# Float32 P·V for two tiles in place of four and a half, in whole 128-row pieces, with exponentials of four tiles kept in PSUM

## The chip, the cores and the metric

One core of a Trainium2 chip. The metric is the device time of one execution in microseconds (us), the median over several runs. Engines are named as in the profile: PE is TensorE, PEld its weight load, DVE is VectorE, ACT is ScalarE, POOL is GpSimd, SP is SyncE, which issues every DMA here.

## What is computed

Attention with rotary positions over 4 batches, 8 heads, 576 rows and 64 columns a head, then a two-layer network with a parametric ReLU on all 2304 rows. All inputs and outputs are float32 (the weights come to the chip as 64-bit words and are converted there).

```python
scores = matmul(rot(q), rot(k).T) / sqrt(64)
attn = exp(scores - max(scores))
attn = attn / (sum(attn) + 1e-09)
x = matmul(attn, v)                       # to [2304, 512]
h = x @ w_in                              # 512 -> 2048
g = maximum(h, 0) + alpha * minimum(h, 0)
out = g @ w_out                           # 2048 -> 512
```

## The kernel before

**Tiles and blocks.** The 2304 rows are 18 tiles of 128 rows, two tiles to a block. A batch has 576 rows, so batch 0 is tiles 0 to 3 and the first half of tile 4 (called 4a here, its other half 4b). Attention of a tile goes by pairs of heads (`pair`): both heads' scores go into two PSUM buffers of the tag `pair` (L766), then each head goes on by itself (`head`): the row maximum on DVE (L814), the exponential with its sum on ACT (L818), and P·V. For a half tile (`half_pair`) the two heads' 64 rows stand in one buffer of 128 partitions, so the work up to P·V is done once for both.

**Two ways for P·V.** Batch 0 goes the float32 way (`head_f32`): five PE transposes write the exponentials back into the same PSUM buffer (L858), a copy on ACT or DVE brings them to SBUF (L868, L869), and five float32 matmuls with 128, 128, 128, 128 and 64 rows give P·V (L863). PE runs each float32 matmul as two instructions, so one head is 10 instructions of L863. The other batches go the split way: P is scaled and written as a float16 part (`p_hi`, L827 on ACT, L829 through the helper of L460 on DVE) and a float16 remainder (`p_lo`, L831, DVE), SP issues a DMA transpose of both (`p_turn`, L835), and 14 float16 matmuls with V's own two parts give P·V (L842). V is split once a batch: its largest value on ACT or DVE (`v_max`), a short chain for the scale (`v_bound`), the parts (`v_hi`, L554, ACT; `v_lo`, L558, DVE) and two small DMAs a pair of heads (`v_shift`). For batch 0 the scale alone is formed, before tile 4.

**The network.** Blocks 0 and 1 run it in float32 (L929 the first layer, L956 the second), with 16 steps j a block. Each j is L929, then on ACT and DVE the activation (L947, L950), then L956. From block 2 on it runs with split float16 weights and inputs (L936, L974). There is one PSUM buffer for a first-layer result, so the next j's first layer waits for L950 of this one.

**What runs beside what.** Attention of tiles 0 and 1 runs alone. Then attention of block i+1 runs beside the network of block i, on the same engines. In blocks 0 and 1 the weights are also loaded (L609), converted by three DVE operations each (L591, L596, L600), and later split into two float16 parts (L669 to L677 and L687 to L691).

**The order.** The whole program is planned ahead: `Plan.run` simulates five engines, and an engine that is free takes the ready operation with the lowest key, which is its due time plus an offset from the tables `OFF` and `PEN`. What an engine executes is fixed in that order, SP's queue included. [...]

**PSUM.** There are three buffers of the tag `pair`, one `v` and one `h`. Beside the network one `pair` buffer holds the second layer's sums and attention has the other two. In the float32 way a buffer is free after the copy of L868 or L869; in the split way after the exponential, which goes to an SBUF buffer `e` (two of them).

Of the kernel before, what the change touches and what calls it, by code (L numbers as in the profile page):

```python
# [37 lines left out]
NB, NF = 1, 2  # L38
# [5 lines left out]
    "a_bound": [34.01],  # L44
    "alpha": [-62.66],
    "beta": [139.98],
    "eps": [-27.34],
    "exp": [79.08, 81.69, -20.81, 118.21, 156.27, -106.7, 113.18, 210.0, -10.34],
    "eye": [-64.76],
    "f_copy": [-31.64, -37.36, -102.13],  # L50
    "f_pv": [4.79, -100.55, 119.9],
    "f_turn": [124.68, -7.54, 47.11],
    "gh": [-121.31, -121.31, -209.6, -195.84, -162.63, -294.46, -186.23, -108.51, 43.31],
    "gl": [-108.2, -108.2, -125.9, -107.83, -164.4, -121.69, -183.9, -105.22, -107.42],
    "k_add": [-6.37, -107.42, -77.63, -62.38],
    "k_hi": [-17.31, 206.39, 65.35, -11.75],
    "k_lo": [-8.45, 101.55, 60.72, -91.74],
    "k_load": [-121.58, -5.26, 126.18, -177.4],
    "k_mul": [60.28, 5.5, 144.31, 120.8],
# [3 lines left out]
    "norm": [-30.88, -90.24, -74.41, -41.63, -82.09, -98.15, -6.94, -46.4, 90.17],  # L63
    "p_hi": [-58.14, -58.14, -74.15, 7.2, -22.71, 28.22, -32.85, -19.97, -141.27],
    "p_lo": [0.78, 0.78, -4.23, -48.72, -107.88, 120.43, -23.33, 100.96, -22.39],
    "p_turn": [-60.56, -60.56, -9.24, -181.49, -122.05, -85.88, -83.8, 1.05, -60.99],
    "prelu": [-103.2, -47.63, -208.13, -158.48, -88.74, -22.37, 44.96, 69.39, 126.15],
    "pv": [-0.07, -0.07, -58.65, 1.14, 35.89, 11.06, -9.72, 3.01, 13.88],
    "q_add": [335.99, 222.46, 352.3, 486.65, 358.5, 547.76, 421.94, 324.24, 183.36, 360.56, 277.59, 215.55, 247.18, 276.04, 353.98, 417.31, 295.01, 298.07],
    "q_hi": [79.07, 79.07, 79.07, 79.07, 79.07, 68.02, 27.89, 98.78, 75.48, 139.53, -68.85, 122.73, 33.74, 111.04, 86.24, 188.84, 327.3, 98.3],  # L70
    "q_lo": [43.6, 43.6, 43.6, 43.6, 43.6, 15.46, -1.52, -47.43, -21.1, 36.88, 86.21, -93.64, -64.6, -97.08, -232.93, -50.34, 94.96, -73.31],
    "q_load": [-36.84, -74.58, -4.21, -63.07, -133.9, -6.27, 8.43, -228.53, -218.75, -128.69, -36.92, -51.96, -68.15, -151.88, -143.73, -53.86, 29.83, 9.38],
    "q_mul": [15.75, -153.47, -6.76, 16.19, 81.64, 140.86, -12.48, 242.35, -145.86, -16.83, -95.05, -56.59, 30.24, 123.99, -64.6, 111.53, 41.76, 19.84],
    "qd_hi": [0.48, 0.48, 83.94, 76.74, 34.0, 32.87, 15.7],
    "qd_lo": [15.84, 15.84, 144.03, 14.21, 12.4, 26.43, 36.9],
    "qd_zero": [-12.23, -12.23, 17.58, 3.62, -12.96, -20.64, -130.84],
    "relu": [19.99, -79.39, -142.28, -117.18, -150.93, -198.12, -66.5, -252.61, -83.53],
    "res": [65.32, 45.86, 121.16, 21.91, 72.49, 6.0, -83.92, -21.55, 69.41],
    "scores": [-8.97, 2.78, -84.49, -37.64, -2.03, -17.61, 11.45, 33.02, -3.31],
    "store": [-82.23, -121.07, -79.43, -39.06, 109.09, 234.19, 235.51, 70.93, 189.03],  # L80
    "tab": [-148.29, -112.05],
    "v_bound": [-167.23, -131.59, -10.65, -88.48],
    "v_hi": [-18.97, -156.9, -74.24, -181.19],
    "v_lo": [-23.23, -55.85, 32.22, 25.69],
    "v_load": [-45.39, 64.43, 42.85, -44.07],
    "v_max": [125.78, 164.73, 111.8, 175.9],
# [1060 lines left out]
```

## Time and profile before

| | us |
|---|---|
| median of 3 runs | 668.09 |
| the runs | 667.92, 668.09, 672.72 |
| the profiled execution | 670.72 |
| its span, first to last instruction | 668.9 |
| PE busy / DVE / ACT / POOL | 631.4 / 486.3 / 356.7 / 235.5 |

The page gives busy time by engine, slices of the span, the chain that ended last, and the costliest groups of instructions. A PE instruction's own duration holds a pipeline tail that overlaps the next one, so the time that a PE group takes is read from its start to the start of the next group. A count is followed by the busy time and the mean of one.

### The profile page before, as it was taken

The numbers are of one execution on the slowest core, as the hardware profiler recorded it, in microseconds if no ns is written. First come the engines' busy times: TensorE is split into PE (matmuls) and PEld (weight loads), VectorE is DVE, ScalarE is ACT, GpSimd is POOL, SyncE is SP. The second block draws the span as 40 slices with busy tenths as digits, with TensorE's granted clock in tenths as the row PEclk, the third lists the DMA queues.
The fourth block names the chain that finished last, engine by engine and source line by source line (L and its number), as shares of the span: only waits on it lengthen the run. The fifth ranks groups of instructions, "written<-read, shape, count | busy, mean of one in ns | idle before, by whom it ended". The sixth has DMA issues, their size and how long they took to land.

```text
span 668.9 us, 13924 instructions
## 1 busy us (share of the span) xinstructions
PE 631.4 (94%) x5482; PEld 451.3 (67%) x5482; DVE 486.3 (73%) x779; ACT 356.7 (53%) x792; POOL 235.5 (35%) x185
## 2 busy tenths in 40 slices
PE   1799899999999999999999999999999999999997
PEld 1578677677676666677766767777667666776664
DVE  5999688524589889887978786689867757853332
ACT  2386555422497665755676555477445555633322
POOL 3767200001077853564855352138621211210000
PEclk9989999999999999999999999999999999999999
DMA  8953555001145876577978586287645828860000
GB/s 307 403 202 115 222 202 190 1 1 31 68 134 135 137 137 105 134 138 150 210 140 193 112 166 110 52 158 172 130 52 105 145 48 115 155 97 1 31 2 33
DMA packets 162130, 84.29 MB, mean 126 GB/s; under 512 B 144912, under 2 KB 148624, under 8 KB 162064
## 3 DMA queue, kind: packets, MB, share of 16 engines
q1 hardware_dynamic: 162064, 83.39, 54.1%
q8 instruction: 43, 0.70, 0.4%
q14 instruction: 23, 0.19, 0.1%
HBM read 41.56 MB, written 4.72 MB: 69 GB/s over the span
## 4 chain that ended last, share of the span: by engine, by line
PE 78%; DMA 8%; DVE 6%; ACT 4%; issue 2%; SPq 1%; DVEq 0%; ACTq 0%
PE h L936 19%; PE pair L974 18%; PE pair L766 8%; PE pair L956 8%; PE h L929 7%; PE v L863 7%; PE v L842 6%; DMA pt<-pp 6%; PE pair L858 3%; PE pair L787 2%; DMA kraw<-in_k_dram 2%; ACT e L818 1%; DVE mx L814 1%; DVE pp L831 1%; DMA out_dram<-os 1%
## 5 line engine op out<-in xcount | busy, mean ns | idle before, releaser
L936 PE MATMUL h<-xt,wi 128*128 128x256 f16 (+1 forms) x1344 | 169.5, 273 | 1.3 <-DVE r L950 1.2
L936 PEld LDWEIGHTS <-wi 128*128 128x128 f16 (+1 forms) x1344 | 127.0, 98 | 34.6 <-issue 5.3
L818 ACT ACTIVATE e<-pair,mx 128x576 f32<-128x576 f32 x144 | 105.6, 737 | 62.7 <-DVE mx L814 56.8
L974 PE MATMUL pair<-wh,gh 128*128 128x512 f16 x448 | 133.4, 379 | 0.3 <-DVE os L460 0.3
L950 DVE SCALAR_TENSOR_TENSOR r<-r,beta,h 128x256 f32<-128x256 f32 x144 | 68.5, 476 | 85.5 <-ACT r L947 84.6
L947 ACT ACTIVATE r<-h 128x256 f32<-128x256 f32 x144 | 54.7, 380 | 131.2 <-PE h L936 86.7
L967 POOL TENSOR_TENSOR gl<-r,gh 128x256 bf16<-128x256 f32 x66 | 57.6, 873 | 168.1 <-ACT gh L964 102.8
L814 DVE TENSOR_REDUCE mx<-pair 128x1 f32<-128x576 f32 x144 | 103.0, 748 | 11.5 <-PE pair L766 9.4
L831 DVE SCALAR_TENSOR_TENSOR pp<-e,pp 128x576 f16<-128x576 f32 x108 | 103.2, 962 | 8.4 <-ACT pp L827 7.7
L974 PE MATMUL pair<-wh,gl 128*128 128x512 f16 x224 | 84.9, 379 | 0.0
L842 PEld LDWEIGHTS <-pt 128*128 128x128 f16 (+1 forms) x1680 | 59.5, 101 | 18.5 <-DMA pt<-pp 8.8
L842 PE MATMUL v<-vv,pt 128*128 128x64 f16 (+1 forms) x1680 | 64.8, 194 | 6.1 <-DMA pt<-pp 4.8
L964 ACT ACTIVATE gh<-r 128x256 f16<-128x256 f32 x100 | 41.5, 415 | 46.7 <-DVE r L950 26.5
L929 PE MATMUL h<-xt,wi 128*128 128x256 f32 x256 | 64.2, 389 | 1.9 <-DVE r L950 1.2
L974 PEld LDWEIGHTS <-gh 128*128 128x128 f16 x448 | 41.2, 98 | 33.7 <-issue 2.1
L956 PE MATMUL pair<-wo,r 128*128 128x512 f32 x128 | 61.4, 602 | 0.0
L863 PEld LDWEIGHTS v<-vf,pt 128*128 128x128 f32 (+3 forms) x400 | 46.8, 179 | 15.6 <-issue 9.0
L929 PEld LDWEIGHTS h<-xt,wi 128*128 128x128 f32 x256 | 46.3, 190 | 13.8 <-issue 4.3
L863 PE MATMUL v<-vf,pt 128*128 128x64 f32 (+3 forms) x400 | 52.5, 272 | 1.2 <-ACT pt L868 1.1
L766 PE MATMUL pair<-kh,qn 64*128 64x288 f32 x576 | 51.3, 308 | 0.5 <-ACT e L818 0.5
L766 PEld LDWEIGHTS pair<-kh,qn 64*128 64x128 f32 x576 | 39.8, 184 | 15.6 <-issue 7.1
L714 POOL TENSOR_TENSOR qr<-qr,tab 128x1024 f32<-128x1024 f32 (+1 forms) x17 | 40.2, 2370 | 22.0 <-DMA qr<-in_q_dram 21.8
(121 smaller groups left out, 749.2 us busy)
## 6 DMA issues: line engine op xcount, KB each, us to landing
qr<-in_q_dram SPq DMA_DIRECT2D x17, 512.0 KB, 4.0
wraw<-in_moe_w_in_dram SPq DMA_DIRECT2D x16, 512.0 KB, 5.9
wraw<-in_moe_w_out_dram SPq DMA_DIRECT2D x16, 512.0 KB, 5.7
kraw<-in_k_dram SPq DMA_DIRECT2D x12, 576.0 KB, 4.8
out_dram<-os SPq DMA_DIRECT2D x18, 256.0 KB, 2.5
vraw<-in_v_dram SPq DMA_DIRECT2D x12, 320.0 KB, 4.3
kraw<-in_k_dram SPq DMA_DIRECT2D x8, 288.0 KB, 4.4
pt<-pp SPq DMA_TRANSPOSE x108, 3.4
```

What stands on the lines that cost most here:

```text
L766: nc.tensor.matmul(out=ps[h]()[:, x, :HS], lhsT=qn()[r, p] if b == 0 else qn()[r, i, p], rhs=kt()[r, c] if b == 0 else kt()[r, j, c], star ...
L814: lambda e: nc.vector.tensor_reduce(out=mx()[a:z], in_=ps()[a:z, :, :HS], axis=AX.XY, op=ALU.max, negate=True),
L818: lambda e: nc.scalar.activation(out=ex()[a:z].rearrange("p (x c) -> p x c", x=2), in_=ps()[a:z, :, :HS], func=ACTF.Exp, bias=mx()[a:z], a ...
L831: lambda e: nc.vector.scalar_tensor_tensor(out=pp()[a:z, 1], in0=ex()[a:z], scalar=E_SC, in1=pp()[a:z, 0], op0=ALU.mult, op1=ALU.subtract),
L842: nc.tensor.matmul(out=v_b()[c:d, 2 * p + g], lhsT=pt()[:, s, o:o + d - c], rhs=vt()[:, g, w], start=(n == 0), stop=(n == len(order) - 1))
L863: nc.tensor.matmul(out=v_b()[c:d, 2 * p + g], lhsT=pt()[:w, s, o:o + d - c], rhs=raw()[:w, g, s], start=(s == 0), stop=(s == NH - 1))
L929: nc.tensor.matmul(out=ps(), lhsT=w32(kk, j // FG)[:, f], rhs=x()[:, kk], start=(kk == 0), stop=(kk == KC - 1))
L936: nc.tensor.matmul(out=ps(), lhsT=wt.bitcast(BF16) if w else wt, rhs=xs.bitcast(BF16) if y else xs, start=(kk == 0 and n == 0), stop=(kk = ...
L950: lambda e: nc.vector.scalar_tensor_tensor(out=g(), in0=g(), scalar=beta_b()[:, j:j + 1], in1=ps(), op0=ALU.mult, op1=ALU.add),
L956: nc.tensor.matmul(out=po()[:, x], lhsT=g()[:, x * 128:(x + 1) * 128], rhs=wf[j // 2]()[:, j % 2], start=(j == 0), stop=(j == KF - 1))
L967: lambda e: ENG[e].tensor_tensor(out=gl(), in0=g(), in1=gh(), op=ALU.subtract),
L974: nc.tensor.matmul(out=po()[:, x], lhsT=s()[:, ts], rhs=w, start=(j == 0 and c == 0), stop=(j == KF - 1 and c == 2))
```

## The change

- `WHOLE = (0, 1)`: only tiles 0 and 1 go the float32 way. Tiles 2, 3 and 4a take the split way for P·V. Their scores stay in float32, and blocks 0 and 1 keep the float32 network, so y of tiles 2 and 3 is transposed by PE as before and their output gets V's scale at the end.
- V of batch 0 is therefore split too (`split_values`), at tile 2; it is loaded into the `vraw` buffers and no longer into `vv` slots.
- The float32 way has five pieces of 128 rows: the last covers the last 128 rows, of which the host lays out a sixth piece of V whose upper half is zero. So its load grows from five pieces to six.
- `IN_PLACE = (2, 3, 4, 5)`: in these tiles the exponential writes back into its PSUM buffer, and `p_hi` and `p_lo` read it there. The buffer is free after `p_lo`. [...]
- The tables `OFF`, `PEN` and the three constants behind them are new, so the order of all operations is another one.
- The case `NB`, which was 1, is taken out; it changes no order by itself.

```diff
-NB, NF = 1, 2
+NF = 2
+WHOLE = (0, 1)
+IN_PLACE = (2, 3, 4, 5)
...
-PW, LW, BACKLOG = 205.88, 49.53, 2091.5
+PW, LW, BACKLOG = 209.82, 40.46, 4570.2
...
-    rv_T = tag("vraw", NP, [128, 2, NH, D], F32)
+    rv_T = tag("vraw", NP, [128, 2, NH + 1, D], F32)
...
-            raw = vraw[b, p] = made(vv_T.new(), vv_T, [128, 2, NH, D], F32, "vf") if b == 0 else rv_T.new()
-            load("v_load", b, at, raw, 128 * 2 * NH * D * 4, raw, v[b, p])
+            n = NH + 1 if b == 0 else NH
+            raw = vraw[b, p] = rv_T.new()
+            load("v_load", b, at, raw, 128 * 2 * n * D * 4, lambda raw=raw, n=n: raw()[:, :, :n], v[b, p][:, :, :n])
...
-        mx, ex, pt = mx_T.new(), e_T.new(), pt_T.new()
+        mx, pt = mx_T.new(), pt_T.new()
+        if t in IN_PLACE:
+            ex, e_y, e_z = ps, lambda: ps()[a:z, :, :HS], lambda y: y.rearrange("p (x c) -> p x c", x=2)
+        else:
+            ex = e_T.new()
+            e_y, e_z = lambda: ex()[a:z], lambda y: y
...
-        if b == 0:
+        if t in WHOLE:
             return head_f32(i, at, t, p, sides, c, d, ex, ps, pt)
...
-        op("p_hi", i, at + 0.2, {ACT: act(S), DVE: dve(S, fast=True)},
+        op("p_hi", i, at + 0.2, {ACT: act(S, t in IN_PLACE), DVE: dve(S, fast=t not in IN_PLACE)},
...
-           reads=[ex, (pp, 0)], writes=[(pp, 1)])
+           reads=[ex, (pp, 0)], writes=[(pp, 1)], port=t not in IN_PLACE)
...
             for s in range(NH):
-                w = min(128, S - 128 * s)
-                nc.tensor.transpose(flat()[:w, 128 * s:128 * s + 128], ex()[:, 128 * s:128 * s + w], eye_b())
+                o = min(128 * s, S - 128)
+                nc.tensor.transpose(flat()[:, 128 * s:128 * s + 128], ex()[:, o:o + 128], eye_b())
...
-                w = min(128, S - 128 * s)
-                nc.tensor.matmul(out=v_b()[c:d, 2 * p + g], lhsT=pt()[:w, s, o:o + d - c], rhs=raw()[:w, g, s],
+                nc.tensor.matmul(out=v_b()[c:d, 2 * p + g], lhsT=pt()[:, s, o:o + d - c], rhs=raw()[:, g, s if s < NH - 1 else NH],
...
-            if t == 2 * NF and a == 0 and p == 0:
+            if t == WHOLE[-1] + 1 and p == 0:
                 bound_values(at, 0, bank().new())
+                split_values(at, 0)
...
+    vt = np.concatenate([vt, np.zeros_like(vt[:, :, :, :, :1])], axis=4)
+    vt[:, :, 64:, :, -1] = vt[:, :, :64, :, -2]
```

## Rows read from the trace of the kernel before

**Rows 1.** The page's first part: busy time, share of the span, instructions.
```profile
span 668.9 us, 13924 instructions
PE 631.4 (94%) x5482; PEld 451.3 (67%) x5482; DVE 486.3 (73%) x779; ACT 356.7 (53%) x792; POOL 235.5 (35%) x185
```

**Rows 2.** By stretch: us; busy PE, PEld, DVE, ACT, POOL; PEclk; DMA share; GB/s.
```profile
17.00:72.00 55.00, 48.57 (x312) 38.46 (x312) 49.98 (x46) 33.04 (x67) 36.51 (x18) 0.97 0.60 232
72.00:178.00 106.00, 104.44 (x540) 75.62 (x541) 63.78 (x94) 44.00 (x92) 5.12 (x9) 1.00 0.29 106
178.00:264.00 86.00, 83.05 (x632) 57.74 (x631) 76.24 (x130) 61.95 (x125) 53.63 (x31) 1.00 0.59 121
264.00:600.00 336.00, 328.68 (x3562) 235.69 (x3560) 264.73 (x443) 193.19 (x451) 133.91 (x119) 1.00 0.69 130
```

**Rows 3.** What PE waited for, whole span: us in total, times, longest.
```profile
PE pair L858 <- ACT e L818: 7.2, 6, 4.2
PE v L842 <- DMA pt<-pp: 4.8, 10, 1.2
```

**Rows 4.** Timeline of PE beside block 0's network: start, us to the last end, group.
```profile
84.41 1.89 PE L929 MATMUL h<-xt,wi 128*128 128x256 f32 x8
86.13 1.25 PE L858 MATMUL pair<-eye,e 128*128 128x128 f32 x10
87.23 1.88 PE L956 MATMUL pair<-wo,r 128*128 128x512 f32 x4
88.94 2.76 PE L863 MATMUL v<-vf,pt 128*128 128x64 f32 x20
91.63 1.99 PE L929 MATMUL h<-xt,wi 128*128 128x256 f32 x8
```

**Rows 5.** That L863 group cut off after 8, 10, 12 and 14 instructions.
```profile
88.94 1.00 PE L863 MATMUL v<-vf,pt 128*128 128x64 f32 x8
88.94 1.36 PE L863 MATMUL v<-vf,pt 128*128 128x64 f32 x10
88.94 1.73 PE L863 MATMUL v<-vf,pt 128*128 128x64 f32 x12
88.94 1.95 PE L863 MATMUL v<-vf,pt 128*128 128x64 f32 x14
```

**Rows 6.** Timeline of PE: split P·V of two heads, and what follows it.
```profile
266.15 0.99 PE L842 MATMUL v<-vv,pt 128*128 128x64 f16 x28
266.97 1.47 PE L936 MATMUL h<-xt,wi 128*128 128x256 f16 x12
```

**Rows 7.** Timeline of PE: float32 P·V of tile 4a's two heads, and what follows.
```profile
174.89 1.80 PE L863 MATMUL v<-vf,pt 128*64 128x64 f32 x20
176.62 1.55 PE L956 MATMUL pair<-wo,r 128*128 128x512 f32 x3
```

**Rows 8.** Groups by shape, whole span: count, busy us, mean ns, idle before and releaser.
```profile
L814 DVE TENSOR_REDUCE mx<-pair 128x1 f32<-128x576 f32 x144 | 103.0, 748 | 11.5 <-PE pair L766 9.4 <-PE pair L787 1.6
L460 DVE TENSOR_SCALAR pp<-e 128x576 f16<-128x576 f32 x44 | 24.2, 553 | 8.5 <-ACT e L818 5.3 <-DMA pt<-pp 2.5 <-ACT gh L964 0.6
L868 ACT ACTIVATE pt<-pair 128x640 f32<-128x640 f32 x30 | 20.6, 703 | 10.4 <-PE pair L858 10.0 <-ACT pt L868 0.2
L558 DVE SCALAR_TENSOR_TENSOR vv<-vraw,vs,vv 128x640 f16<-128x640 f32 x12 | 13.0, 1091 | 0.0
L869 DVE COPY pt<-pair 128x640 f32<-128x640 f32 x6 | 4.9, 809 | 0.6 <-PE pair L858 0.6
```

**Rows 9.** Line L831 (`p_lo`): minimum/median/maximum ns; then its group in 178 to 264 us.
```profile
L831 DVE SCALAR_TENSOR_TENSOR pp<-e,pp x108: 705/758/2935, 207.1 to 590.2; 128x576 f16<-128x576 f32 x108
L831 DVE SCALAR_TENSOR_TENSOR pp<-e,pp 128x576 f16<-128x576 f32 x17 | 20.3, 1201 | 3.1 <-ACT pp L827 2.9
```

**Rows 10.** The page's DMA issues: count, median us from issue to landing.
```profile
pt<-pp SPq DMA_TRANSPOSE x108, 3.4
```

**Rows 11.** Busy time by stretch, as in rows 2: the stretch with the lowest clock.
```profile
30.00:40.00 10.00, 8.56 (x52) 6.51 (x49) 10.00 (x7) 6.74 (x14) 10.00 (x4) 0.83 0.74 276
```

More of the change, by code (lines that the diff above doesn't have):

```diff
@@ new lines @@
+    "gl": [-56.66, -56.66, -65.53, -99.05, -167.22, -76.19, -61.37, -23.5, -20.2],
+    "k_add": [-10.96, -33.09, -97.86, 0.73],
+    "k_hi": [-55.86, 187.0, 126.74, 36.14],
+    "k_lo": [2.38, 117.68, 88.59, -61.9],
+    "k_load": [-161.85, -73.74, 145.38, -367.4],
+    "k_mul": [-50.45, 14.06, 209.81, 96.88],
[3 rows of a table added]
+    "norm": [-189.28, -226.95, -291.49, -279.05, -424.65, -168.92, -147.92, -316.46, -185.99],
+    "p_hi": [-72.55, -80.2, -226.05, -45.39, -90.15, 34.88, -152.84, -41.6, -68.84],
+    "p_lo": [-31.52, -58.13, -17.16, 0.89, -225.67, 96.95, -38.03, 155.76, -95.5],
@@ L881, in normalise @@
         whole = t < 2 * NF
-        by = None if whole else vs[0] if b == 0 else 1.0 / (E_SC * X_DOWN)
+        by = 1.0 / (E_SC * X_DOWN)
         op("y", i, at, {DVE: dve(DM)},
-           lambda e: nc.vector.tensor_tensor(out=y()[a:z], in0=vo()[a:z], in1=wide(), op=ALU.mult) if whole
-           else nc.vector.scalar_tensor_tensor(out=y()[a:z], in0=vo()[a:z], scalar=by()[a:z] if b == 0 else by, in1=wide(),
+           lambda e: nc.vector.tensor_tensor(out=y()[a:z], in0=vo()[a:z], in1=wide(), op=ALU.mult) if t in WHOLE
+           else nc.vector.scalar_tensor_tensor(out=y()[a:z], in0=vo()[a:z], scalar=by, in1=wide(),
                                                op0=ALU.mult, op1=ALU.mult),
-           reads=[rs] + [(vo, (h, a)) for h in range(H)] + ([vs[0]] if b == 0 and not whole else []), writes=[(y, a)], port=False)
+           reads=[rs] + [(vo, (h, a)) for h in range(H)], writes=[(y, a)], port=False)
         if whole:
@@ L992, in result @@
                     continue
-                if b not in xw:
+                if i >= NF and b not in xw:
                     xw[b] = xw_T.new()
@@ L1049, in attention @@
                     split_values(at, b)
-            if t == 2 * NF and a == 0 and p == 0:
+            if t == WHOLE[-1] + 1 and p == 0:
                 bound_values(at, 0, bank().new())
+                split_values(at, 0)
             pair(*(u[0:3]), *u[3:], [bank(), bank()])
     bound_alpha()
-    for i in range(NB):
-        attention(i)
+    attention(0)
     for g in range(NG):
         weights(g)
-    attention(NB)
-    po = [pair_T[i].new() for i in range(NB)]
-    for j in range(KF):
-        for i in range(NB):
-            expert(i, j, po[i])
-    for i in range(NB):
-        result(i, po[i])
-    for i in range(NB, len(blocks)):
-        if i > NB:
-            attention(i)
+    for i in range(len(blocks)):
+        if i < 1 or i > 1:
+            attention(max(i, 1))
         po = pair_T[0].new()
```

212 lines of the change are left out of this document (100 added, 112 removed), and 6 rows, old and new, of the table OFF.

## The prediction

> **What bounds the kernel now.** I read the page's first part first: PE is busy 94% of the span, DVE 73%, ACT 53%, POOL 35% [rows 1]. A busy PE need not be the bound, so the second view is busy time by stretch [rows 2]. While tiles 0 and 1 run alone (17 to 72 us) DVE is busy 50.0 of 55 us and PE 48.6. Beside block 0's network (72 to 178) PE is busy 104.4 of 106 and DVE only 63.8, POOL 5.1. Beside block 1's network (178 to 264) both are full: PE 83.1 of 86, DVE 76.2. After that (264 to 600) PE has 328.7 of 336. The third view is what PE waited for: 7.2 us for exponentials and 4.8 us for DMA transposes in the whole span [rows 3]. So from 72 us on the end is set by how much PE has to do. What the change takes from PE there comes off the time, as long as DVE, which gets part of the work, keeps up.
>
> **What leaves PE.** The timeline beside block 0 gives the price of a pair of heads, from each start to the next [rows 4]. Transposes: 87.23 - 86.13 = 1.10 us. Float32 P·V: 91.63 - 88.94 = 2.69 us. The same P·V, cut off after 8, 10, 12 and 14 instructions, shows where that goes [rows 5]: the step from 12 to 14 is one full piece, 0.22 us; from 8 to 10 is the 64-row piece, 0.36; from 10 to 12 is the full piece behind it, 0.37. So a short last piece costs 0.14 and 0.15 more, and behind the pair's second head the 0.15 falls on the instruction after it: 2.69 + 0.15 = 2.84 us for two heads.
>
> Tiles 2 and 3 have eight pairs. Each loses 1.10 + 2.84 = 3.94 us and gets the split P·V of two heads, 266.97 - 266.15 = 0.82 us [rows 6]. That is 3.12 a pair, 25.0 us in all.
>
> Tile 4a has four pairs, each transposed once (0.55 us). Its P·V takes 176.62 - 174.89 = 1.73 us [rows 7], with the switch behind it 1.88. Less 0.82 that is 1.61 a pair, 6.4 us.
>
> Tiles 0 and 1 keep float32 P·V, in ten full pieces a pair: 2.84 - 10 x 0.22 = 0.64 us, eight times, 5.1 us. A 128-row last piece isn't in the trace. It can't be cheaper than the other full pieces (0.22) and I see no reason for more than the 64-row one (0.36), at which the gain is nothing; I take 0.22, since it is then just another full piece.
>
> Sum on PE: 36.5 us.
>
> **What arrives elsewhere.** On DVE, 20 more `p_lo` (16 for tiles 2 and 3, 4 for 4a), now read from PSUM. That operation isn't in the trace. From SBUF it has a minimum of 0.705 and a median of 0.758 us [rows 9]; the maximum over as many PSUM elements takes 0.748, a PSUM copy of 640 elements 0.809 [rows 8]. I take 0.75 between bounds of 0.71 and 0.81: 15.0 us, 12.0 of it beside block 0. V's four remainders at 1.09 add 4.4. Of 36 copies of transposed exponentials 6 were on DVE [rows 8]; 20 go, so about 3 of 0.81, 2.2 of it beside block 0. There DVE comes to 63.8 + 12.0 + 4.4 - 2.2 = 78.0 us, in a stretch that shrinks to 106 - 25 = 81. That is 96%, more than the 91% and 89% that DVE reached in the stretches on either side [rows 2]. What should relieve it is POOL, busy 5.1 us there: a few us of DVE's K and Q work may be planned on POOL. So I cost this at nothing, and without that relief DVE at 91% needs 85.7 us, 4.7 lost.
>
> The 20 new `p_hi` (and the 12 of tiles 4b and 5) may go to ACT or DVE. ACT is busy 44.0 of 106 us and loses most of the copies at 0.703, so it has room. On DVE a `p_hi` from SBUF takes 0.553; from PSUM I scale the copy, 0.809 x 576/640 = 0.73 [rows 8]. With before's share (44 of 108) 13 of the 32 would be on DVE and cost 13 x 0.18 = 2.3 us more.
>
> [...]
>
> Tiles 4b and 5 gain on DVE. Their `p_lo` in 178 to 264 averages 1.20 us against a minimum of 0.705 [rows 9], with POOL busy 53.6 us beside it. [...]
>
> The exponential written to PSUM isn't in the trace either. Between 0 and 0.2 us to either side for each of 32, it is ACT's, and ACT is never above 72% in these stretches, so nothing on the path.
>
> Keeping a PSUM buffer until `p_lo` holds it for `p_hi` and `p_lo`, some 1.45 us, where the float32 way held it for transpose and copy, 0.55 + 0.70. That is 0.2 longer, 20 times, at most 4 us if the next scores wait each time; for tiles 4b and 5, which released it after the exponential, 1.45 on eight sets of scores, 11.6. Eight pairs over 81 us leave ten us to each, so I take nothing; the network fills PE meanwhile.
>
> V of batch 0 now has to be split before tile 2's first P·V. Queued behind it on ACT and DVE are the exponentials and maxima of that tile. If none of it were hidden, the four remainders and their ACT parts would cost about 8 us once; V is loaded before tile 0's first P·V, long before tile 2, so I take nothing. Its load grows by 64 KB four times, 0.26 MB at 232 GB/s [rows 2], 1.1 us while DMA is a bound. I pay that in full. SP also issues 20 more transposes and 8 shifts, among them in the order the weight loads; DMA share beside block 0 is 0.29, so there is room.
>
> **The sum.** Of the 25.0 us beside block 0 I take off the idle share that PE has where DVE is as full, 7.3 of 336 us [rows 2] or 1.8 in 81: 23.2. Of tile 4a's 6.4 I keep 5, of the 5.1 in tiles 0 and 1, where DVE is as full as PE, 3. Together 31.2, less 1.1 for V's load: 30.1. The profiled execution has a span of 668.9 us and took 670.7; the median of the runs is 668.1. The span should come to 638.8 and the median to 638.0.
>
> **The rivals.**
> Gain kept, as above, 630 to 645 us: chance 0.66. Below 630, where the new order also gets back some of the 12 us of PE's waits [rows 3] on top of 36.5: 0.03.
>
> DVE becomes the bound beside blocks 0 and 1. For it: 96% by my own sum. [...] If ACT takes `p_hi`, 4.7 us are lost, 643; if `p_hi` is on DVE as well, 78.0 + 16 x 0.73 = 89.7 at 91% needs 98.6 us in place of 81, 17.6 lost, 656. 645 to 657: chance 0.20.
>
> PE's clock falls beside block 0. In the stretch in which PE waits most, the granted clock averaged 0.83 over 10 us [rows 11], part of it at the lower of the two levels, which costs 1.7 us. If each of the eight pairs brought such a dip, 13.6 us would go: 652. Against: 1.00 in every later stretch, also where split attention and network alternate. Chance 0.03. [...]
>
> Slower than before: the 20 new transposes stand on PE's path. One takes 3.4 us from issue to landing [rows 10]. If PE waited for each in full, 68 us would come on top, 706. It decides from 30.1/20 = 1.5 us of PE idle a transpose. Against: 4.8 us for all 108 now, 0.04 each, longest 1.2 [rows 3]. For: weight loads share the queue while tile 2 runs. Chance 0.04. That gain and losses cancel to within 1%, by holding the PSUM buffers (15.6) and DVE (17.6) together: 0.04.
>
> **Chances and range.** A measurement of this kernel tells about 1% from no change. Faster by over 1% (below 661.4): 0.66 + 0.03 + 0.20 + 0.03 = 0.92; within 1% 0.04; slower 0.04. The range is 630 to 650: the forecast, the nearer half of the DVE case, together about 0.8.
>
> **What would show it.** PE's first L936 at about 234 us, where it now stands at the border of 264; L863 with 160 instructions at 2.2 us a pair, all with 128 rows; L858 with 80; 24 more groups of L842; DVE about 90% beside block 0 with PE still above 95%; `p_lo` near 0.75 in tiles 2 to 5. The forecast is wrong if PE shows waits on `p_lo`, transposes or free PSUM buffers of more than a few us before 234, or if the stretch after the first L936 is no longer about 405 us.

## The result, and the profile after

The changed kernel takes 647.61 us (median of 4 runs, 646.35 to 649.58), the kernel before 670.40 on the same chip (4 runs, 667.92 to 672.89): ratio 0.966, 95% interval 0.961 to 0.972. It is faster, within the range of 630 to 650, but 9.6 us above the forecast of 638.0. The profiled execution took 646.35 us with a span of 644.6, against 670.72 and 668.9.

The page's first part, which answers [rows 1], and busy time by stretch, which answers [rows 2] (us; busy PE, PEld, DVE, ACT, POOL; PEclk; DMA share; GB/s):

```profile
span 644.6 us, 14003 instructions
PE 603.8 (94%) x5478; PEld 427.6 (66%) x5478; DVE 498.4 (77%) x819; ACT 355.5 (55%) x794; POOL 210.9 (33%) x172
...
17.00:72.00 55.00, 47.46 (x322) 39.41 (x321) 53.80 (x60) 35.28 (x69) 37.94 (x19) 0.93 0.56 207
72.00:160.00 88.00, 84.60 (x582) 54.99 (x582) 77.46 (x115) 49.76 (x107) 13.96 (x14) 0.96 0.84 220
160.00:245.00 85.00, 84.07 (x686) 58.20 (x685) 76.86 (x140) 56.55 (x116) 37.35 (x24) 1.00 0.63 134
245.00:580.00 335.00, 325.24 (x3484) 233.84 (x3481) 259.33 (x440) 190.43 (x449) 118.39 (x107) 1.00 0.67 126
```

PE still has 94% of a shorter span, DVE went from 73% to 77%. From 72 to 160 us DVE is busy 77.5 of 88 us and POOL 14.0. Some 7 us at the end of that stretch belong to block 1 already; in block 0 itself (69.4 to 153.1) it is DVE 74.4 of 83.7 us, 89%, and POOL 9.7, where POOL had 5.1. The mean granted clock (PEclk) tells something new: it was 1.00 beside block 0 and is 0.96, and 0.97 before the network and is 0.93.

The sharper cut is where each block's network begins, the first group of its first layer. All times are spans of profiled executions; two more executions of the changed kernel (r_after, r_after2, below) show how far such a number varies.

| stretch | before | after | repeats | forecast | measured |
|---|---|---|---|---|---|
| to block 0 (tiles 0, 1) | 72.0 | 69.4 | 70.4, 71.3 | -1.9 | -0.8 to -2.6 |
| block 0 | 99.3 | 83.7 | 85.2, 84.0 | -23.2 | -14.1 to -15.6 |
| block 1 | 92.4 | 83.4 | 86.2, 86.1 | -5.0 | -6.2 to -9.0 |
| from block 2 to the end | 405.2 | 408.0 | 407.5, 406.0 | 0 | +0.8 to +2.8 |
| span | 668.9 | 644.6 | 649.3, 647.3 | -30.1 | -19.6 to -24.3 |

So the gain is there, 24.3 us in the first execution, and what is missing is missing beside block 0. What PE did in that block, each instruction counted from its start to the next one's start less idle time: transposes 9.7 (0.6 of it for tile 4a's first pair) and float32 P·V 21.4 us left (31.1), split P·V came (7.1). But the first layer, whose instructions are the same, went from 29.2 to 32.8 us, the scores of whole tiles from 8.3 to 9.4, the second layer from 26.3 to 26.9: 5.3 us more for the same work. Four sets of half-tile scores moved in from block 1 (+1.0), idle time rose from 1.5 to 3.4, and y's transposes took 0.2 more. -24.0 + 5.3 + 1.0 + 1.9 + 0.2 = -15.6. Of the 5.3, 3.7 stand in the stretches at the lower clock (0.50 granted); the other 1.6 stand at full clock (1.00), where a first-layer instruction takes 234 ns for 228 and one of the second layer 449 for 438 (one right behind split P·V 513).

The timeline of PE where block 0 begins shows both losses (start, us to the last end, group, and in brackets the idle time before it and what ended it):

```profile
67.11 0.66 PE L904 MATMUL v<-eye,y 128*128 128x128 f32 x4 [0.85 <-DVE y L891]
69.42 3.78 PE L936 MATMUL h<-xt,wi 128*128 128x256 f32 x8 [1.65 <-ACT xt L908]
73.13 2.37 PE L769 MATMUL pair<-ks,qp 64*128 64x288 f32 x8
76.52 1.13 PE L936 MATMUL h<-xt,wi 128*128 128x256 f32 x4 [1.02 <-DVE r L957]
78.83 0.93 PE L850 MATMUL v<-vv,pt 128*128 128x64 f16 x14 [1.18 <-DMA pt<-pp]
```

The first group of L936 takes 3.78 us where such a group takes 1.99 at full clock [rows 4]. What PE did before the clock fell stands in short stretches of the same execution (columns as above), first of after, then of before:

```profile
50.00:54.00 4.00, 3.85 (x28) 3.25 (x28) 4.00 (x4) 2.45 (x5) 4.00 (x3) 1.00 0.02 4
54.00:58.00 4.00, 3.54 (x16) 2.94 (x18) 4.00 (x3) 2.53 (x6) 3.43 (x3) 0.57 0.00 0
...
66.00:70.00 4.00, 1.50 (x8) 1.04 (x8) 4.00 (x5) 4.00 (x9) 2.17 (x2) 0.78 0.68 197
70.00:74.00 4.00, 4.00 (x11) 2.90 (x11) 4.00 (x6) 0.75 (x2) 0.00 (x0) 0.50 0.50 122
74.00:78.00 4.00, 2.63 (x11) 1.54 (x9) 2.17 (x4) 1.38 (x4) 0.00 (x0) 0.87 1.09 308
78.00:82.00 4.00, 3.17 (x30) 2.43 (x31) 2.86 (x5) 3.97 (x10) 0.00 (x0) 0.57 1.25 199
```

```profile
70.00:74.00 4.00, 3.33 (x19) 2.13 (x15) 4.00 (x3) 1.11 (x2) 3.92 (x2) 1.00 0.05 20
74.00:78.00 4.00, 2.45 (x19) 1.96 (x18) 3.97 (x6) 3.69 (x9) 0.57 (x1) 1.00 0.52 180
```

From 66 to 70 us PE was busy 1.50 of 4, while DVE and ACT were full, and then the granted clock was 0.50 (cut into single microseconds, from 17 us to the end, both executions show 1.00 or 0.50, and a value between only where it changes). Before, the same handover from tile 1 to block 0 kept PE busy at least 2.45 of 4, with tile 2's transposes and float32 P·V among it, and the clock stayed at 1.00. So the work that the change takes from PE was also part of what kept it busy there. That PE mostly waited fits this fall alone. Ahead of the one at 78.5 us PE was busy 2.63 of 4, more than the 2.45 of before, whose clock stayed; ahead of the one at 54.6 us it was busy 3.85.

### The profile page after: what moved, and what is told of

Same layout as the page of the kernel before. It is cut to its first block, busy times and chain, and to the rows that moved or that the text cites. A ratio compares the mean times of both kernels' runs of the same rounds, so it can differ in the third digit from the quotient of the medians.

```text
span 644.6 us, 14003 instructions
## 1 busy us (share of the span) xinstructions
PE 603.8 (94%) x5478; PEld 427.6 (66%) x5478; DVE 498.4 (77%) x819; ACT 355.5 (55%) x794; POOL 210.9 (33%) x172
## 4 chain that ended last, share of the span: by engine, by line
PE 67%; DVE 12%; DMA 12%; ACT 4%; issue 3%; SPq 1%; POOL 1%; ACTq 0%; DVEq 0%
PE pair L981 19%; PE h L943 19%; PE v L850 7%; PE pair L769 7%; DMA pt<-pp 6%; PE h L936 5%; PE pair L963 4%; DVE mx L822 2%; DMA wraw<-in_moe_w_in_dram 2%; PE pair L866 2%; PE pair L790 2%; DVE wh L694 1%; DVE pp L839 1%; ACT e L826 1%; PE v L870 1%
## 5 line engine op out<-in xcount | busy, mean ns | idle before, releaser
L943 PE MATMUL h<-xt,wi 128*128 128x256 f16 (+1 forms) x1344 | 166.3, 273 | 2.3 <-DVE r L957 1.9
L826 ACT ACTIVATE e<-pair,mx 128x576 f32<-128x576 f32 x112 | 82.1, 736 | 50.2 <-DVE mx L822 47.2
L974 POOL TENSOR_TENSOR gl<-r,gh 128x256 bf16<-128x256 f32 x59 | 49.4, 838 | 157.2 <-ACT gh L971 116.9
L839 DVE SCALAR_TENSOR_TENSOR pp<-e,pp 128x576 f16<-128x576 f32 x96 | 83.1, 873 | 7.5 <-ACT pp L835 6.4
L850 PEld LDWEIGHTS <-pt 128*128 128x128 f16 (+1 forms) x2016 | 70.9, 102 | 25.6 <-DMA pt<-pp 13.6
L850 PE MATMUL v<-vv,pt 128*128 128x64 f16 (+1 forms) x2016 | 77.9, 194 | 7.6 <-DMA pt<-pp 7.3
L971 ACT ACTIVATE gh<-r 128x256 f16<-128x256 f32 x103 | 42.7, 414 | 48.5 <-PE pair L981 31.5
L936 PE MATMUL h<-xt,wi 128*128 128x256 f32 x256 | 66.1, 399 | 3.1 <-ACT xt L908 1.6
L936 PEld LDWEIGHTS h<-xt,wi 128*128 128x128 f32 x256 | 48.5, 196 | 21.9 <-DVE r L957 7.9
L717 POOL TENSOR_TENSOR qr<-qr,tab 128x1024 f32<-128x1024 f32 (+1 forms) x16 | 38.0, 2376 | 23.5 <-DMA qr<-in_q_dram 23.5
L974 DVE TENSOR_TENSOR gl<-r,gh 128x256 bf16<-128x256 f32 x53 | 25.4, 478 | 26.0 <-ACT gh L971 26.0
L981 PEld LDWEIGHTS <-gl 128*128 128x128 bf16 x224 | 21.9, 98 | 27.2 <-POOL gl L974 0.8
```

Source lines behind the costliest of these rows:

```text
L826: lambda e: nc.scalar.activation(out=e_y() if t in IN_PLACE else e_y().rearrange("p (x c) -> p x c", x=2), in_=ps()[a:z, :, :HS], func=ACT ...
L839: lambda e: nc.vector.scalar_tensor_tensor(out=e_z(pp()[a:z, 1]), in0=e_y(), scalar=E_SC, in1=e_z(pp()[a:z, 0]), op0=ALU.mult, op1=ALU.sub ...
L850: nc.tensor.matmul(out=v_b()[c:d, 2 * p + g], lhsT=pt()[:, s, o:o + d - c], rhs=vt()[:, g, w], start=(n == 0), stop=(n == len(order) - 1))
L936: nc.tensor.matmul(out=ps(), lhsT=w32(kk, j // FG)[:, f], rhs=x()[:, kk], start=(kk == 0), stop=(kk == KC - 1))
L943: nc.tensor.matmul(out=ps(), lhsT=wt.bitcast(BF16) if w else wt, rhs=xs.bitcast(BF16) if y else xs, start=(kk == 0 and n == 0), stop=(kk = ...
L974: lambda e: ENG[e].tensor_tensor(out=gl(), in0=g(), in1=gh(), op=ALU.subtract),
```

## The experiments

Every kernel here but e3_old_order replays a planned order written out as a list, so that an edit moves nothing else; an entry is name.block.number (of the batch for V, of the quarter for weights), `...` stands for entries left out, and the number of the engine at the end of each is left out too. The first two are the changed kernel itself in that form, for comparison.

**r_after and r_after2: the changed kernel, replayed.** No edit but the list.

> The changed kernel with its order written out as a list, so that later kernels can change one thing and keep the order of all else. Every theory: the same time as the changed kernel, 646 to 650 us, with PE's granted clock at the lower level for some 14 us between 54 and 82 us.

> The changed kernel with its order written out, once more, as the one to compare the next three with on the same chip. Every theory: 646 to 650 us.

Measured: 649.38 us, ratio 0.967 (0.962 to 0.972), and 649.31, ratio 0.965 (0.961 to 0.969). In r_after PE waited 3.08 us for y of tile 1, not 0.85 (3.14 in r_after2), since one weight conversion on DVE took 3.37 us (3.43 in r_after2, 1.23 in after):

```profile
61.26 1.21 DVE L705 SCALAR_TENSOR_TENSOR wo<-wraw,wo 128x1024 int32<-128x1024 int32 x1
...
63.30 3.37 DVE L701 SCALAR_TENSOR_TENSOR wo<-wraw,wo 128x1024 int32<-128x1024 int32 x1
...
67.92 0.68 DVE L993 TENSOR_TENSOR y<-v,rs 128x512 f32<-128x512 f32 x1
```

Beside block 0, where POOL is busy 9.7 of 83.7 us in after, such conversions take 1.21 to 1.23 us. POOL's product for tile 5's Q stood beside this one in both executions: in r_after it began first, at 63.22 us, and took 2.36; in after it began second, at 63.51 against the conversion's 63.45, and took 3.39. So in each the one that began second took the longer time. By such things block 0 begins 1.0 and 1.9 us later here than in the execution shown above.

**e1_pieces: the 128-row pieces alone.** The kernel before in its own order, with the last piece of the transposes and of the float32 P·V widened to 128 rows and the sixth piece of V loaded.

```diff
-                w = min(128, S - 128 * s)
+                o = min(128 * s, S - 128)
...
-                lhsT=pt()[:w, s, o:o + d - c], rhs=raw()[:w, g, s]
+                lhsT=pt()[:, s, o:o + d - c], rhs=raw()[:, g, s if s < NH - 1 else NH]
```

> The kernel before, in its own order, with one part of the change alone: float32 P·V and its transposes in five pieces of 128 rows in all of batch 0. By the price of 0.64 us a pair (0.29 a head): eight pairs each beside tiles 0 and 1 and beside block 0, where PE is the bound only in the latter: 5.1 us off beside block 0, 0.3 a head for tile 4a, up to 2.3 us, and 0 to 3 of 5.1 us alone with tiles 0 and 1; 5 to 10 us under the kernel before in all. If a 128-row last piece cost as much as the 64-row one (0.36 us), nothing comes off.

Measured: 669.9 us, ratio 0.9947 (0.9921 to 0.9973), 3.5 us, less than the 5 to 10 expected. The pair costs what [rows 5] gave as the lower bound:

```profile
90.93 2.34 PE L962 MATMUL v<-vf,pt 128*128 128x64 f32 x20
93.11 1.95 PE L1028 MATMUL h<-xt,wi 128*128 128x256 f32 x8
```

93.11 - 90.93 = 2.18 us, 2.69 in [rows 4]. Beside block 0 P·V went from 21.4 to 17.6 us and the stretch from 99.3 to 95.0. Before block 0 nothing came of it (74.4 us in place of 72.0, and P·V itself 22.8 us for 22.3): there PE isn't alone in setting the time.

**e2_not_in_place: exponentials in SBUF again.** After's program and order, but tiles 2 to 5 write their exponentials to SBUF.

```diff
-IN_PLACE = (2, 3, 4, 5)
+IN_PLACE = ()
```

> Order of the changed kernel, but tiles 2 to 5 write the exponential to an SBUF buffer again, as all later tiles do, and their float16 parts are read from there. Theory A and B: keeping it in PSUM saved contention of the remainder with POOL and cost the fast form of the first part, on engines that are not the bound; within 2 us of the changed kernel, DVE's remainder averaging over 0.80 us in tiles 4b and 5 in place of 0.75. Theory C (DVE is the bound beside blocks 0 and 1): 3 to 8 us slower. Theory D (a PSUM buffer held until the remainder is done delays scores): 2 to 5 us faster.

Measured: 653.36 us, ratio 0.972 (0.967 to 0.977), 4.0 us slower than r_after (652.6 to 655.7 us against 648.3 to 653.1). That is the time which theory C gave (3 to 8 us), where A and B had at most 2; but it comes beside block 1 alone. Block 0 takes 84.2 us, as in after; block 1 91.4 where the repeats have 86.2 and 86.1. The groups by shape beside block 1, of e2_not_in_place and of r_after2 (count, busy us, mean ns, idle before):

```profile
L941 DVE SCALAR_TENSOR_TENSOR pp<-e,pp 128x576 f16<-128x576 f32 x17 | 18.4, 1095 | 0.4 <-ACT pp L937 0.2
```

```profile
L941 DVE SCALAR_TENSOR_TENSOR pp<-pair,pp 128x576 f16<-128x576 f32 x14 | 10.3, 746 | 0.1
...
L941 DVE SCALAR_TENSOR_TENSOR pp<-e,pp 128x576 f16<-128x576 f32 x4 | 3.8, 965 | 0.3 <-ACT pp L937 0.2
```

`p_lo` takes 1.10 us from SBUF (e2) and 0.75 from PSUM (r_after2) where POOL is busy beside it, 44.0 of 91 us and 42.2 of 86, and DVE is busy 80.3 of 91 us there in e2; beside block 0, where POOL is busy 9.7 of 83.7 us in after, it averages 0.83 for 0.75 and the block takes no longer. So beside POOL's work `p_lo` is the slower one with both inputs in SBUF, and not with one in PSUM; why is not shown.

**e3_old_order: the new program in an order planned from the tables of before.**

(Shortened: the tables' entries are not printed.)

```diff
-OFF, PEN, PW, LW, BACKLOG = (the new tables)
+OFF, PEN, PW, LW, BACKLOG = (the tables of before)
```

> After's program with the order planned from the tables of offsets and penalties of before (the planner itself, its costs and the new steps are after's). It tells what planning anew was worth. Theory (parts alone): the program's gain of some 22 us stands for the most part, and the new order is worth 0 to 6 us, ratio .967 to .976. Rival (the new order carries the gain): without it the ratio is .98 or more, over 9 us of the gain.

Measured: 681.10 us, ratio 1.010 (1.000 to 1.021). The rival holds, by more than it said: without its own order the program isn't faster at all, 31.7 us slower than in r_after, on another chip. Block 0 begins at 80.1 us, blocks 0 and 1 take 88.9 and 95.4, and PE is idle 9.2 us beside block 1. What PE waited for from 60 to 270 us (us in total, times, longest):

```profile
PE v L850 <- DMA pt<-pp: 8.0, 3, 3.8
PE v L904 <- DVE y L891: 2.5, 1, 2.5
PE h L936 <- DVE r L957: 2.1, 2, 1.3
PE v L850 <- DMA vv<-vv: 2.1, 1, 2.1
```

Transposes, which the forecast costed at nothing, stand at the top: 3.8 us of it is the first transpose of tile 2. The wait for V's parts (vv) comes at 181.6 us and is for batch 1's V, not for the new split. These waits are less than what is lost; the granted clock (0.93 from 74 to 168 us) and the start of block 0 come on top. The old tables were fitted to other operations, so this doesn't price planning anew by itself; it shows that the saving on PE arrives only with an order that fits it. The reverse, the kernel before in a newly fitted order, was not run; beside block 0 another order had little to win there, as PE idled 1.5 of 99.3 us at a clock of 1.00.

**e4_filler: PE kept busy at the handover.** Six dummy matmuls before and behind y's transposes of tile 1; their results are not used.

```diff
+for _ in range(n):      # n = 2 before, 4 behind
+    nc.tensor.matmul(out=buf(), lhsT=eye_b(), rhs=tab_b()[:, 0, :256], start=True, stop=True)
```

> Order of the changed kernel; six float32 matmuls of 256 columns, whose results nobody reads, are added on PE where it idles between tile 1 and the network (two before the transposes of tile 1's y, four behind). Nothing else is changed. Theory A (what is missing beside block 0 is PE's clock, which falls because PE idles there): the clock stays up from 68 to 82 us, the first L936 group takes 1.9 us in place of 3.8 and the scores behind it 1.25 in place of 2.4, and 3 to 6 us come off. Theory B (PE waits there for V's parts and the first transposes of tile 2 whatever its clock): the matmuls get shorter, but the first L850 still starts at about 79 us, and at most 1 us comes off. Theory C (DVE is the bound beside block 0): no change.

Measured: 650.07 us, ratio 0.967 (0.962 to 0.972), as r_after. PE on the timeline, then 64 to 72 and 72 to 80 us by stretch:

```profile
69.86 1.96 PE L1049 MATMUL h<-xt,wi 128*128 128x256 f32 x8 [0.15 <-PE h L1010]
...
73.66 1.23 PE L871 MATMUL pair<-ks,qp 64*128 64x288 f32 x6 [1.15 <-DVE pp L941]
78.16 2.07 PE L1049 MATMUL h<-xt,wi 128*128 128x256 f32 x4 [3.27 <-DVE r L1070]
...
64.00:72.00 8.00, 7.85 (x44) 5.97 (x44) 7.64 (x9) 6.96 (x14) 4.38 (x2) 1.00 0.45 124
72.00:80.00 8.00, 3.58 (x12) 1.90 (x11) 4.83 (x8) 1.81 (x5) 0.00 (x0) 0.70 0.77 206
```

The first layer's first group now takes 1.96 us at full clock. Then PE waits 3.27 us for the activation r and the clock falls there. So keeping the clock up at the first wait gains nothing: PE came sooner to a wait that was there anyway, and the clock fell at that one. Theory A's case, a clock that stays up to 82 us, did not arise.

**e5_split_early: V of batch 0 split before the last weight conversions.** The split's operations go from the handover to where tile 1's last exponentials are copied.

```diff
-... f_copy.0.14 f_copy.0.15 ... v_hi.0.0 ... v_lo.0.0 ... l1.0.0 v_lo.0.1 ... v_lo.0.3
+... f_copy.0.14 v_hi.0.0 v_lo.0.0 v_shift.0.0 v_shift.0.1 f_copy.0.15 v_hi.0.1 ... v_shift.0.7 ... l1.0.0
```

> Order of the changed kernel, except that V's scale and the splitting of batch 0's V are moved ahead by about 4 us: on DVE and ACT ahead of the weight conversions that stood before them, on SP ahead of tile 2. Theory B (V's splitting stands on PE's path at the start of tile 2): the first transposes of tile 2 go out about 3 us earlier, the first L850 starts at about 76 us in place of 79, and 2 to 6 us come off, part of it by a higher clock. Theory A (the clock alone): at most 2 us, as the idle time between tile 1 and the network, 66 to 69 us, stays. Theory C (DVE is the bound beside block 0, at 88%): no change, since DVE has the same work to do.

Measured: 650.14 us, ratio 0.967 (0.962 to 0.972). Block 0 takes 80.6 us, the shortest of all, but begins at 76.7: PE waits 8.3 us for y of tile 1, which now stands behind the split on DVE. Block 1 so begins at 157.3 us, 1.6 later than in r_after (155.7).

**e6_queue: the transposes first in SP's queue.** Batch 1's V loads and maxima go behind tile 2, one weight load behind the first transposes.

```diff
-... v_load.1.0 ... wo_load.1.1 ... v_load.1.1 ... p_turn.1.0 ... v_max.1.0 ... relu.0.0 ... p_turn.1.1
+... p_turn.1.0 ... relu.0.0 ... p_turn.1.1 wo_load.1.1 ... p_turn.1.7 v_load.1.0 v_load.1.1 v_load.1.2 v_load.1.3
```

> Order of the changed kernel, except that batch 1's V loads and their maxima on ACT (not needed before 120 us) stand behind tile 2 and not ahead of its first transposes, and one weight load stands behind the first two transposes. Theory E (the first transposes of tile 2 wait in the DMA queue behind those loads, and the first activation waits on ACT behind a maximum whose load hasn't landed): the first two transposes land in 3.5 to 4.5 us in place of 5.2 and 6.1, the first L850 group starts at 76 to 77.5 us in place of 78 to 79, the clock dips there shorten, and 2 to 4 us come off beside block 0. [...]

In after, the first two transposes are issued behind loads of V and a weight and land 5.27 and 6.09 us later; the activation of the first j stands on ACT behind a maximum of batch 1's V, which waited 4.07 us for its load. Here the transposes land in 3.30 and 3.28, and that activation comes at once. Beside block 0 PE waits 0.3 us for transposes, 4.6 in r_after2. Measured all the same: 657.0 us, ratio 0.976 (0.972 to 0.981), 7.7 us slower than r_after2, where theory E had 2 to 4 us less. The timeline shows where it went:

```profile
79.33 0.69 DVE L696 TENSOR_SCALAR wo<-wraw 128x1024 int32<-128x1024 int32 x1 [4.68 <-DMA wraw<-in_moe_w_out_dram]
...
82.70 0.39 ACT L1056 ACTIVATE r<-h 128x256 f32<-128x256 f32 x1
...
84.73 3.78 PE L1038 MATMUL h<-xt,wi 128*128 128x256 f32 x8 [3.99 <-DVE r L1059]
```

DVE stands 4.68 us before a conversion whose weight load this edit held back, everything behind it is late, PE waits 3.99 us, and the next group takes 3.78 us for 1.99 at full clock [rows 4]. At 122 us the same happens once more (3.45 us, and 3.78 for the group): four V loads now stand ahead of three weight loads in SP's queue, and these land 6.0 to 8.1 us after their issue. So the loads in the queue are shown to be what the transposes wait for; what their wait alone costs isn't, as the edit brought waits for r of 7.4 us in its place (0.5 in r_after2).

**e7_handover: e6 with tile 5's Q on POOL moved later too** (and one more weight load), so that no POOL product runs beside the conversions before y.

```diff
-... q_mul.5 ... q_add.5 ... wo_load.1.3 ... p_turn.1.3 ...
+... p_turn.1.3 wo_load.1.3 ... qd_zero.2.1 q_mul.5 q_add.5 ...
```

> As the kernel before it in this list, and besides POOL's product and sum for tile 5's queries (not needed before 150 us) stand behind tile 2's start, and a second weight load behind the next two transposes. [...] Theory E: no faster than the one with the loads alone. [...]

Measured: 658.45 us, ratio 0.979 (0.975 to 0.983). The wait for y is down to 0.94 us, block 0 still takes 94.2, with a wait of 4.91 us for r: DVE stood 4.98 us before a conversion, for its weight load, as in e6.

**e8_no_vlo: the split's DVE part left out.** The low half of batch 0's V isn't computed.

```diff
+            if b == 0:
+                op("v_lo", b, late, {POOL: gps(2 * NH * D)},
+                   lambda e, t=t: nc.gpsimd.memset(t()[:, :, NSEG:], 0.0), writes=[(t, 1)])
```

> After's program in after's order, but the low half of batch 0's V is not computed: the four DVE operations of about 1.2 to 2 us each are left out at the handover from tile 1 to block 0, and POOL writes zeros there once, early (so tiles 2 and 3 are computed without the low half of V). Theory D (DVE's queue at the handover is what costs: it is busy without a break from 44 to 72 us, and the V split stands in it): the first wait for y of tile 1 and the waits for the first prelu shrink, block 0 begins about 2 us earlier or is shorter by 3 to 5 us, the ratio to before falls from .966 to about .960 (4 us). Rival E (something else is late there, the loads ahead of the first transposes or the clock): the end moves by under 1.5 us, ratio .964 to .967.

Measured: 648.73 us, ratio 0.961 (0.953 to 0.970), which the interval doesn't tell from after. Block 0 begins no earlier (71.5; PE still waits 3.12 us for y, a DVE result) and takes 81.4 us, 2.3 to 3.8 less than after's three. Block 1 begins at 152.9, 0.2 to 2.8 us earlier than in after's three. That is the order of what V's remainders on DVE cost block 0, as far as single executions tell; the theory's 4 us for the whole is not shown.

**e9_conv_late: weight conversions out of the handover.** Five conversions of w_in's second quarter go from tile 1's time into block 0.

```diff
-... wi_conv.1.1 ... wi_conv.1.5 ... wo_conv.0.2 ... wo_conv.0.4 ... l1.0.0 ...
+... wo_conv.0.1 ... wo_conv.0.5 ... l1.0.0 ... l1.0.1 wi_conv.1.1 ... prelu.0.0 wi_conv.1.2 ... relu.0.1 wi_conv.1.5
```

> After's program with another order: five weight conversions of the second quarter of w_in (wi_conv 1.1 to 1.5, about 1.2 us of DVE each) go from the time of tile 1 to the first 15 us of block 0, where their result is not needed before layer 1's ninth group; the conversions of w_out's first quarter take their places. Nothing else moves but one weight load that waits for them. Theory D: DVE has about 5 us less before block 0 begins and five more inside it, where it has some 10 us of idle time; if that idle time is real, block 0 begins 2 to 4 us earlier and the ratio is .961 to .964. Rival (DVE is the limit of tile 1 and block 0 taken together, as the early V split suggested): the start moves and block 0 grows by the same, ratio .966 to .970.

Measured: 648.28 us, ratio 0.964 (0.956 to 0.971). The wait for y is 0.85 us (after's three have 0.85, 3.08 and 3.14), block 0 begins at 70.9, within after's 69.4 to 71.3, and takes 86.0, with 5.7 us idle. Block 1 begins at 156.9, no earlier than in after's three (153.1, 155.7, 155.2). The interval doesn't tell the theory's time from the rival's.

**e10_spread: e9, V split pair by pair, V loads one by one.**

```diff
-... v_hi.0.1 ... v_lo.0.1 v_load.1.0 ... v_lo.0.2 ... v_lo.0.3 ... l1.0.2
+... p_turn.1.1 v_load.1.0 ... pv.1.1 v_lo.0.1 ... p_turn.1.3 v_load.1.1 ... p_lo.1.4 v_lo.0.2 ... p_lo.1.5 v_lo.0.3
```

> After's program in an order meant to be better at the handover: the conversions of w_out's first quarter come before block 0 and five of w_in's second quarter inside it; of batch 0's V only the first pair of heads is split before tile 2, the others some 10 to 25 us later, each before its own product; batch 1's V loads and their maxima follow the first transposes one by one. Theory D (what DVE, ACT and SP hold in the first 10 us of block 0 makes the waits there): the transposes of tile 2 land in about 3.5 us, PE idles under 2 us in block 0 in place of 3.4, the clock stays up, ratio .955 to .961, that is 3 to 7 us faster than after. Rival (DVE is so full beside tile 1 and block 0 that an operation moved out of one place is late in another): waits of about the same sum appear later in block 0, ratio .964 to .970.

Measured: 652.17 us, ratio 0.970 (0.965 to 0.975): the rival. Block 0 begins first of all, at 68.1 us, and takes 89.7:

```profile
66.79 0.66 PE L1006 MATMUL v<-eye,y 128*128 128x128 f32 x4 [0.85 <-DVE y L993]
...
78.00 0.93 PE L952 MATMUL v<-vv,pt 128*128 128x64 f16 x14 [2.80 <-DMA pt<-pp]
...
94.46 3.21 PE L1038 MATMUL h<-xt,wi 128*128 128x256 f32 x8 [3.19 <-DVE r L1059]
```

In place of one bad start there are waits at 78 and 94 us. That at 94 is r again: its two operations stood behind a maximum and a part of V on ACT and V's remainder on DVE, all of them moved there by this order.

## Why the prediction was right, and where it was short

**The number is inside the range, in part by luck.** The forecast's own case, the gain kept, had 630 to 645 us. 647.6 lies above that, in the 645 to 657 of the rival in which DVE becomes the bound; the range went up to 650 on account of that rival, whose reason did not occur beside block 0. And a miss of 7.6 us there (up to 9.1 in the repeats) was partly made up by 1.2 to 4.0 us in block 1 that the forecast did not have.

**What PE loses: right.** 24.0 us net beside block 0 against 25.0; transposes and float32 P·V 31.1 us (31.5 by the sum), split P·V 7.1 (6.6). Tile 4a lost 5.4 us net where the sum has 6.4, since split P·V of its half heads takes 1.03 us a pair and was costed at 0.82. In float32 a pair now takes 48.74 - 46.46 = 2.28 us, forecast 2.2:

```profile
46.46 2.44 PE L870 MATMUL v<-vraw,pt 128*128 128x64 f32 x20
48.74 0.93 PE L866 MATMUL pair<-eye,e 128*128 128x128 f32 x7
```

The counts that were named came too: L870 (then L863) has 160 instructions, L866 (then L858) 80, and the first split layer begins at 236.6 us, forecast about 234.

**What arrives elsewhere: right in size.** The operations that no trace of before showed, in groups by shape beside block 0 (72 to 160 us):

```profile
L839 DVE SCALAR_TENSOR_TENSOR pp<-pair,pp 128x576 f16<-128x576 f32 x19 | 13.9, 746 | 0.0
...
L462 DVE TENSOR_SCALAR pp<-pair 128x576 f16<-128x576 f32 x5 | 3.8, 753 | 1.2 <-ACT pair L826 1.1
```

`p_lo` 0.746 us, forecast 0.75 out of 0.71 to 0.81; `p_hi` on DVE 0.753, forecast 0.73. The exponential written to PSUM takes 0.707 on ACT, to SBUF 0.736: no cost. From SBUF a `p_hi` on DVE took 0.553 [rows 8], so from PSUM it takes 1.36 times as long. With 11 of 32 `p_hi` on DVE the price was 11 x 0.20 = 2.2 us, forecast 2.3 for 13 of them.

**DVE beside block 0: the relief came.** 74.4 of 83.7 us, 89%, forecast about 90%; POOL took 9.7 us for 5.1. As an average DVE isn't the bound there. Beside block 1 e2 points that way: without the exponentials in PSUM the kernel is as much slower as the theory of DVE as the bound said.

**The step that failed: the first transposes and V's split, costed at nothing.** The forecast took nothing for the transposes because PE had waited 0.04 us for each, and nothing for the split ("about 8 us once" if none of it were hidden) because V is loaded early. But beside block 0 PE waits 2.1 us for transposes in after and 4.6 in each of the repeats, where before had no such wait. The longest of PE's waits in after from 60 to 160 us, then in r_after from 55 to 100 (us in total, times, longest):

```profile
PE v L850 <- DMA pt<-pp: 2.1, 3, 1.2
```

```profile
PE v L952 <- DMA pt<-pp: 4.4, 3, 2.4
```

Up to 234 us it is 6.9 us in r_after, which is more than the few us that the forecast named as the sign of being wrong. How it starts, in after:

```profile
66.38 0.68 DVE L891 TENSOR_TENSOR y<-v,rs 128x512 f32<-128x512 f32 x1
66.97 1.96 DVE L561 SCALAR_TENSOR_TENSOR vv<-vraw,vs,vv 128x640 f16<-128x640 f32 x1
...
70.39 0.75 DVE L839 SCALAR_TENSOR_TENSOR pp<-pair,pp 128x576 f16<-128x576 f32 x1
...
71.49 0.59 SPq L455 DMA_DIRECT2D vraw<-in_v_dram  x1
72.13 0.60 SPq L612 DMA_DIRECT2D wraw<-in_moe_w_out_dram  x1
...
72.83 0.58 SPq L455 DMA_DIRECT2D vraw<-in_v_dram  x1
...
73.51 4.28 SPq L843 DMA_TRANSPOSE pt<-pp  x2
```

The first `p_lo` is done at 71.1 us, but SP issues three loads before its transpose, which lands 5.27 us after its issue. With the loads behind it (e6) it lands in 3.30. The split doesn't wait for V's load; it waits for its turn on DVE, which is busy 53.8 of the 55 us from 17 to 72. Its remainders (L561) stand behind y of tile 1, among tile 2's first `p_hi` and `p_lo`, and ahead of the next conversion and the first prelu. With the remainders earlier (e5) or left out (e8) block 0 takes 80.6 and 81.4 us in place of 83.7 to 85.2. So both had a price; how much of the 7.6 us missing in block 0 is due to either is not shown. In the execution shown the 7.6 are 5.3 of slower instructions (3.7 at the lower clock, 1.6 at full clock), 1.0 of scores that came over from block 1, 1.0 less on PE than forecast, and 0.3 of small terms; the idle share that I took off, 1.8 us, came as 1.9. In the repeats more of it is idle time, which grew by 4.4 and 3.8 us, while the same work took 4.3 and 4.1 longer, 3.2 and 2.4 of it at the lower clock.

**The rival on the clock: it came, in another place.** I gave it 0.03, because later stretches keep 1.00 while attention and network alternate. They do; the dips don't come with the eight pairs but mostly with the handover: 10.2 us at 0.50 between 68 and 82 in after, 6.8 between 67 and 77 in the repeats, and 3.4 at 91.5 in r_after. My ground for the rival was misread: [rows 11] is the stretch with the lowest clock, not the one in which PE waits most. From 70 to 80 us PE was busy less, at a full clock:

```profile
70.00:80.00 10.00, 7.78 (x52) 5.89 (x50) 8.13 (x8) 6.01 (x12) 4.49 (x2) 1.00 0.42 153
```

Nor is the dip a cause by itself: with PE kept busy (e4) the clock fell at the next wait (1.00 from 64 to 72 us, 0.70 from 72 to 80). In after the fall at 68 us stands behind PE's 1.50 busy of 4 us, the one at 54.6 behind 3.85 of 4; so no one amount of waiting ahead of a fall is shown.

**Tiles 0 and 1: about as forecast.** P·V went from 22.3 to 19.2 us there, 3.1 for the 5.1 of the sum, and the stretch by 0.8 to 2.6, forecast 3 less 1.1. But e1 gained nothing before block 0. DVE is busy 53.8 of 55 us there; that it sets the pace is likely, not shown.

**Block 1: more than forecast, 6.2 to 9.0 us for 5.** What `p_lo` of tiles 4b and 5 saves on DVE by reading PSUM, 12 x (1.20 - 0.75) = 5.4 us with the mean of [rows 9], stands in no term of the sum. e2 shows what reading PSUM is worth: without it block 1 takes 91.4 us, 5.2 more than in the repeats and only 1.0 less than before.

**The rest: +0.8 to +2.8, forecast 0.** PE waits 4.0 us for three transposes from 236 to 362 us in after (2.6 in that stretch before); a planned order has its own small waits.

**The rival that ends slower.** It didn't occur, but e3 shows that it was nearer than 0.04: with the order of other tables the same program is as slow as before or slower, and transposes are the largest of its waits from 60 to 270 us.

**What stays open.** Six kernels that change the handover (e4 to e7, e9, e10) end between 0.964 and 0.979, none clearly below after. Most removed the wait at which they were aimed, and another came up; so the waits at the handover are bound up with each other, and no single one is shown to be the cause. Why the clock fell at 54.6 and 78.5 us stays open too. Whether an order exists that gets the 7.6 us back was not settled; a version that beats the changed kernel and computes the whole was not found.

## What to carry to other kernels

An operation that is "hidden" needs a turn in its engine's queue at the moment when it is due: where one phase hands over to the next, look at the queue of every engine in that window and not at the average of the stretch. Work that is taken from the bounding engine also kept it busy at times when it had little else; ask what it will wait for there. Dummy work in its place gained nothing here (e4). And a saving on the bounding engine is worth what the order around it lets through: the same arithmetic in an order made for other operations gained nothing.

## What the runs showed of the hardware

A weight conversion on DVE, with both inputs in SBUF, took 3.37 us where a POOL product had begun 0.08 us ahead of it (r_after). In after, where the product began 0.06 us behind it, it took 1.23, and the product 3.39 in place of 2.36. Beside block 0 such conversions took 1.21 to 1.23. `p_lo` with both inputs in SBUF took 1.10 on average beside block 1, POOL busy 44.0 of 91 us (e2), and 0.75 with one input in PSUM, POOL busy 42.2 of 86 (r_after2). In before, from SBUF, its median was 0.76 and its minimum 0.705 [rows 9]; `p_hi` on DVE took 0.75 from PSUM (after) and 0.55 from SBUF (before). The first DMA transposes took 3.3 us from issue to landing with the loads moved behind them (e6) and 5.3 to 6.1 behind loads in the same queue (after). Making the last 64-row piece a full one, with an input that is partly zero, took a pair from 2.69 [rows 4] to 2.18 us (e1): the half piece was the dearer one.
